# One more slot tile of each destination block fetched from DRAM by node number, with 18 gathered tiles in place of 20

## The chip, the cores and the metric

The kernel runs on one NeuronCore of a Trainium2 chip. The metric is the device time of one execution in microseconds (us), lower is better; the figure is the median of three runs. Beside it stands one execution taken with the hardware profiler, from which every duration comes. TensorE is called PE here, its weight loads PEld; VectorE is DVE, ScalarE is ACT, GpSimd is POOL and SyncE is SP.

## The reference

A graph of 10,000 nodes and 160,000 edges, 128 features a node. Seven propagations (hops) along the edges make seven further tokens of each node, and a small attention block reads the eight tokens out.

```
N, E, D, K = 10000, 160000, 128, 7
h = x; toks = [x]
for _ in range(K):
    msg = h[src] * deg_inv_sqrt[src, None] * deg_inv_sqrt[dst, None]
    h = segment_sum(msg, dst, N)
    toks.append(h)
tok = stack(toks, axis=1)               # (N, 8, D)
# one self-attention block over the 8 tokens of a node (layernorm, q, k, v, softmax, wo, residual),
# then a softmax readout over the tokens with w_r
```

src and dst are drawn at random and uniformly over the nodes.

## The kernel before

**Hops as dense matmuls.** The nodes are cut into 79 blocks of 128. A hop goes over the 79 destination blocks. The edges of one destination block are sorted into cells by the block of their source node; a cell has 32 slots (CAP), a group of four cells makes a slot tile of 128 slots, and 80 cells (NS) make 20 slot tiles (NJ). The edges that don't fit, up to 128 of a destination block, are the left-over edges.

For a destination block t (function `block`), `gather` makes two slot tiles at a time in a PSUM buffer p: for each cell one matmul of a one-hot matrix of 128 x 32 (in w, fp8) against the source block of the table in SBUF (tab, 128 x 256 in f16, the high and low parts of the values). These are L442, eight for a p, 80 for a block; four that lie side by side fill the 128 partitions of a slot tile. ACT or DVE casts p to an SBUF buffer e (L445, ten a block; `evac` says which engine: ACT six and DVE four in hops 2 to 7, ACT all in hop 1). `scat` then adds each slot tile into acc with a one-hot matrix of 128 x 128 (L426, 20 a block).

The left-over edges come another way: POOL issues an indirect DMA (L418), which fetches 128 rows of the table's copy in DRAM (tabd) by the node numbers in oidx into a tile og, and `over` adds it to acc with the one-hot matrix Sov (L432). Then DVE sums the two halves of acc to s (L434) and `fin` runs: in hops 2 to 6 the next table's rows (L559 on ACT, L560 and L562 on DVE) and their write to tabd, issued from ACT's queue (L563), in all hops the scaled token r on POOL (L461) and its write from SP (L463). The fetches of a hop read the whole of the table that the hop before wrote.

**Order.** The program hangs each block's scatters and its `over` on a list `pend` and takes them off two behind, so that the last two scatters and `over` of a block run behind the gathers of the next. The framework then orders the instructions of each engine when the kernel is built, by the program's order and its own estimate of what is ready, and adds all semaphores; an instruction that needs a buffer waits until the buffer's last reader is done. In hops 2 to 7 there are six p buffers, two acc, four og, five w, four s and r; in hop 1 three p, two acc, two og, one s and one r.

**Before and beside hop 1.** Pass A (`pass_a`) sorts the edges into a table TT by destination block (one-hot matrices of 80 columns on DVE, matmuls); `decode` takes the numbers out of TT: kB the cell, sl the node within its source block plus one, dl the destination within its block. In hop 1, `place` sorts the edges of four destination blocks into cells (oh and ux on DVE, 40 pairs of blocks), and `matrices` builds w for each block: DVE compares a broadcast row of source numbers (rb, read back from srow in DRAM) with the partition number for the gather half of w (L403), and the destination numbers dsl with a row of numbers for the scatter half (L406); w is kept in DRAM (GSd) and loaded again in hops 2 to 7 (L568). The matrices of later blocks are built beside hop 1 over the earlier ones.

If an edge is lost, the count of `missing` edges is above zero and a slow path (`slow_hops`, seven loops of 1250 steps with indirect DMAs) computes all tokens anew. After the hops `attention` reads the tokens.

Of the kernel before, what the change touches and what calls it, by code (L numbers as in the profile page):

```python
# [19 lines left out]
NT = 79  # L20
NS = 80
# [4 lines left out]
CAP = 32  # L26
NJ = NS // 4
# [6 lines left out]
class Hops:  # L34
    def __init__(self, ctx, dp, missing, tc, x, src, dst, dis):
# [4 lines left out]
        self.GSd = [dp.tile([128, NJ * 256], F8, name=f"gsd{t}") for t in range(NT)]  # L40
# [3 lines left out]
        self.srow = dp.tile([NS, NS * CAP], F16, name="srow")  # L44
# [48 lines left out]
        self.tab = [cp.tile([128, NS, 256], F16, name=f"tab{i}") for i in range(2)]  # L93
# [7 lines left out]
        self.oidx = cp.tile([128, NT], I32, name="oidx")  # L101
# [116 lines left out]
    def pass_a(self):  # L218
        tc, nc, V, A, T, G = self.tc, self.nc, self.nc.vector, self.nc.scalar, self.nc.tensor, self.nc.gpsimd
        with ExitStack() as c:  # L220
# [33 lines left out]
            for ch in range(NCH):  # L254
                oh, U = st
                U2 = wp.tile([128, NS, 2], F16, name="U2")
                A.activation(U2, U[:, :, None].to_broadcast([128, NS, 2]), AF.Copy)  # L257
# [3 lines left out]
                o12 = w1.tile([128, NP, 2 * NS, 2], F16, name="o12")  # L261
                self.times(o12[:, :, :NS], oh, D1[:, ch])
                self.times(o12[:, :, NS:], oh, D2[:, ch])
# [3 lines left out]
                ta = pp.tile([128, 2, NS], F32, name="ta")  # L267
# [3 lines left out]
                V.tensor_reduce(self.TT[:, ch], ta.rearrange("p h k -> p k h"), axis=X, op=ALU.add)  # L271

    def decode(self):
# [139 lines left out]
    def block(self, t, w, tab, tabd, pend, lag, runs, first, evac, fin):  # L413
# [9 lines left out]
        def scat(e, jj):  # L423
            for j in range(2):
                J = 2 * jj + j
                T.matmul(acc[:, :m], w[:, (NJ + J) * 128:(NJ + J + 1) * 128], e[:, j, :m], start=J == 0, stop=False)  # L426
# [576 lines left out]
```

## Time and profile before

| what | us |
|---|---|
| median of three runs | 4508.32 (4507.62 to 4515.4) |
| the profiled execution, its own time | 4508.36 |
| its span in the trace, first to last instruction | 4506.6 |
| pass A ends, decode begins | 506.2 |
| first gather of hop 1 | 582.6 |
| last matmul of hop 1 | 1370.1 |
| last matmul of hop 7 | 3664.5 |

All stage times are counted from the start of the span. Durations in the text are of this one execution; its own time is 0.04 us from the median. A row of a group reads: line, engine, operation, what is written and read, shapes, count, then busy us and the mean ns of one, then the idle time of the engine ahead of them and what ended it. A timeline row reads: start us, length us, engine, line, operation, count; in brackets the idle time ahead of it and what ended that.

### The profile page before, as it was taken

To read this page: it belongs to the slowest core of one execution; us is meant where nothing else is said; L and a number is where in the kernel's file an instruction comes from. 1 tells how busy PE (TensorE), PEld (TensorE's weight loads), DVE (VectorE), ACT (ScalarE), POOL (GpSimd) and SP (SyncE) were. 2 spreads that over 40 slices of the span, in tenths; PEclk is the share of its full clock that TensorE was granted. 3 is DMA by queue.
4 is the path that set the end of the run, shared out by engine and by line. 5 is a ranking of instruction groups with operands and counts; after the bars stand their busy time and mean duration, and the time that the engine had idled before them with its cause. 6 is when DMAs were issued, how large, how long until landed. Compare 5 with 4: busy or idle time off the path is not lost.

```text
span 4506.6 us, 170913 instructions
## 1 busy us (share of the span) xinstructions
PE 4015.8 (89%) x74352; PEld 3266.3 (72%) x74352; DVE 3529.0 (78%) x7740; ACT 2521.5 (56%) x5159; POOL 1256.0 (28%) x1423
## 2 busy tenths in 40 slices
PE   0566389999998999999999999999999989999996
PEld 0456366766766888888888888888888867777774
DVE  5888799999996777777777777777766668888887
ACT  3000036565666777777777777777766645544542
POOL 0000024334343333333333333333333322222221
PEclk9887689999998999999999999999999989999998
DMA  3000044454455555555555555555555541221210
GB/s 115 1 1 1 1 132 149 140 155 149 142 154 187 182 180 177 183 185 183 178 182 181 179 182 184 177 184 184 181 163 169 164 128 52 65 63 56 65 56 10
DMA packets 296789, 588.20 MB, mean 131 GB/s; under 512 B 46895, under 2 KB 198541, under 8 KB 290781
## 3 DMA queue, kind: packets, MB, share of 16 engines
q1 hardware_dynamic: 218893, 509.90, 34.3%
q0 software_dynamic: 17696, 36.28, 3.8%
q10 hardware_dynamic: 59440, 31.03, 2.4%
q8 instruction: 582, 9.54, 0.8%
q14 instruction: 178, 1.46, 0.1%
HBM read 447.66 MB, written 129.38 MB: 128 GB/s over the span
## 4 chain that ended last, share of the span: by engine, by line
PE 51%; DVE 32%; issue 9%; DMA 4%; POOL 2%; ACT 1%; SPq 1%; ACTq 0%; DVEq 0%; POOLq 0%
PE p L442 20%; PE acc L426 20%; PE ta L270 3%; DVE w L406 3%; DVE st L859 3%; DVE st L856 2%; DVE o L183 2%; DVE w L403 2%; DMA rb<-srow 2%; DVE ro L265 2%; PE tb L335 1%; POOL r L461 1%; DVE R L183 1%; DVE oh L177 1%; DVE ux L190 1%
## 5 line engine op out<-in xcount | busy, mean ns | idle before, releaser
L445 ACT CAST eb<-p 128x512 f16<-128x512 f32 x3634 | 1859.9, 607 | 738.9 <-PE p L442 723.6
L445 DVE CAST eb<-p 128x512 f16<-128x512 f32 x1896 | 1180.2, 683 | 461.3 <-PE p L442 460.7
L442 PE MATMUL p<-tab,w 128*32 128x256 f16 x44240 | 1426.2, 274 | 30.1 <-ACT eb L445 14.3
L426 PE MATMUL acc<-eb,w 128*128 128x256 f16 (+1 forms) x11060 | 1409.4, 274 | 3.1 <-DVE indeg L483 3.0
L442 PEld LDWEIGHTS <-w 128*32 128x32 fp8e4 x44240 | 1118.1, 96 | 268.2 <-issue 185.4
L418 POOL DMA_INDIRECT og<-tabd,oidx x553 | 620.4, 1122 | 2217.8 <-PE acc L432 1426.1
L426 PEld LDWEIGHTS <-w 128*128 128x128 fp8e4 x11060 | 1019.2, 98 | 270.5 <-issue 156.4
L461 POOL TENSOR_SCALAR r<-s,ctok 128x128 f32<-128x128 f32 x553 | 451.2, 816 | 341.4 <-DVE indeg L483 170.5
L560 DVE SCALAR_TENSOR_TENSOR tab<-s,c,tab 128x128 f16<-128x128 f32 x395 | 139.2, 352 | 182.5 <-ACT tab L559 181.1
L434 DVE TENSOR_REDUCE s<-acc 128x128 f32<-128x256 f32 x553 | 234.2, 423 | 41.2 <-PE acc L432 30.7
L406 DVE TENSOR_TENSOR w<-dsl,iof 128x2560 fp8e4<-128x2560 f16 x79 | 222.5, 2816 | 1.2 <-ACT dsl L351 1.2
L257 ACT ACTIVATE U<-U 128x160 f16<-128x160 f32 x25 | 7.6, 304 | 384.5 <-PE U L250 384.5
L768 PEld LDWEIGHTS pv<-Wv,xT 128*128 128x128 f32 x1250 | 165.1, 192 | 75.7 <-issue 57.0
L780 PEld LDWEIGHTS po<-v,pT 128*128 128x128 f32 x1250 | 164.4, 192 | 74.8 <-issue 74.8
L270 PE MATMUL ta<-o,ro 128*128 128x160 f16 x1250 | 132.0, 284 | 93.3 <-DVE ro L265 93.3
L781 ACT COPY o<-po 128x512 f32<-128x512 f32 (+1 forms) x157 | 91.8, 584 | 210.9 <-PE po L780 210.9
L270 PEld LDWEIGHTS <-ro 128*128 128x128 f16 x1250 | 127.0, 121 | 97.4 <-DVE ro L265 97.0
L559 ACT ACTIVATE tab<-s,c 128x128 f16<-128x128 f32 x395 | 158.6, 401 | 62.0 <-DVE s L434 7.4
L748 ACT COPY xT<-pt 128x512 f32<-128x512 f32 (+1 forms) x157 | 91.1, 580 | 166.0 <-PE pt L747 165.9
L768 PE MATMUL pv<-Wv,xT 128*128 128x130 f32 x1250 | 165.8, 276 | 0.0
L780 PE MATMUL po<-v,pT 128*128 128x128 f32 x1250 | 165.1, 275 | 0.0
L250 PE MATMUL U<-oh,tri 128*128 128x80 f16 x1250 | 62.2, 221 | 114.7 <-DVE oh L177 114.7
(245 smaller groups left out, 4291.4 us busy)
## 6 DMA issues: line engine op xcount, KB each, us to landing
w<-gsd SPq DMA_DIRECT2D x474, 640.0 KB
rb<-srow SPq DMA_DIRECT2D x79, 640.0 KB
gsd<-w SPq DMA_DIRECT2D x79, 640.0 KB
tok<-r SPq DMA_DIRECT2D x546, 64.0 KB
x<-tok SPq DMA_DIRECT2D x273, 128.0 KB
tabd<-tab ACTq DMA_DIRECT2D x395, 64.0 KB
og<-tabd,oidx POOLq DMA_INDIRECT x553, 4.0
x<-in_x SPq DMA_DIRECT2D x39, 128.0 KB
```

The source lines that it names most:

```text
L270: T.matmul(ta, ro[:, j, :, i], o12[:, j, :, i], start=j + i == 0, stop=j + i == NP)
L406: V.tensor_tensor(w[:, NJ * 128:].rearrange("p (j d) -> p j d", d=128), dsl[:, g, :, None].to_broadcast([128, NJ, 128]), self.iof1[:, None ...
L418: G.indirect_dma_start(out=og, out_offset=None, in_=tabd, in_offset=bass.IndirectOffsetOnAxis(ap=self.oidx[:, t:t + 1], axis=0))
L426: T.matmul(acc[:, :m], w[:, (NJ + J) * 128:(NJ + J + 1) * 128], e[:, j, :m], start=J == 0, stop=False)
L434: V.tensor_reduce(s, acc[:, 0:256].rearrange("p (h d) -> p d h", h=2), axis=X, op=ALU.add)
L442: T.matmul(p[32 * q:32 * q + 32, j], w[:, s * CAP:(s + 1) * CAP], tab[:, s, :], start=True, stop=True)
L445: (A.copy if evac(jj) else V.tensor_copy)(e[:, :, 0:256], p.rearrange("p j h d -> p j (h d)"))
L461: self.nc.gpsimd.tensor_scalar(r, s, ct[:, t:t + 1], None, op0=ALU.mult)
L559: A.activation(new[:, t, 0:128], s, AF.Copy, scale=c1[:, t:t + 1])
L560: V.scalar_tensor_tensor(new[:, t, 128:256], s, c1[:, t:t + 1], new[:, t, 0:128], op0=ALU.mult, op1=ALU.subtract)
L768: T.matmul(p[:, g - a, :], S[i]["xT"][:, g, :], Wv, start=True, stop=True)
L780: T.matmul(p[:, g - a, :], PT[i % 2][:, g, :], S[i]["v"][:, g, :128], start=False, stop=g == b - 1, skip_group_check=True)
```

## The change

Of the 20 slot tiles of a destination block, 18 (NG) are gathered as before; they hold the source blocks 0 to 71, node numbers below 9216. One tile (NI) holds the remaining 784 nodes in four cells of some 196 nodes, and its rows are fetched from tabd by node number, with an indirect DMA of its own (og0) beside that of the left-over edges (og1). There are so 76 cells, nine gathers and evictions a block, 18 scatters, and a matmul of the fetched tile, `fetched`, which stands behind the block's first scatter, or in `over` for block 0. Its matrix is the 19th of the scatter half of w, which now comes first in w. acc is taken at the first scatter. The og buffers are two of each kind in place of four. In hop 1 `fetched` has a second matmul of one column, which counts degrees. `decode` works out the cell and the node number within it; `place` sums the node numbers of the fetched tile into PSUM with four small matmuls a block and converts them to oidx on DVE. Pass A works with 79 columns (NK). ACT does five evictions of a block, DVE four.

```diff
 NT = 79
-NS = 80
+NG = 18
+NI = 1
+CELL = 334
+NK = 79
 CAP = 32
-NJ = NS // 4
+NJ = NG + NI
+NS = 4 * NJ
...
-        self.GSd = [dp.tile([128, NJ * 256], F8, name=f"gsd{t}") for t in range(NT)]
+        self.GSd = [dp.tile([128, (NJ + NG) * 128], F8, name=f"gsd{t}") for t in range(NT)]
         self.tabd = [dp.tile([NT * 128, 256], F16, name=f"tabd{i}") for i in range(2)]
-        self.srow = dp.tile([NS, NS * CAP], F16, name="srow")
+        self.srow = dp.tile([NTP, 4 * NG * CAP], F16, name="srow")
...
-        self.oidx = cp.tile([128, NT], I32, name="oidx")
+        self.oidx = cp.tile([128, NT, NI + 1], I32, name="oidx")
...
-        m, k = oh.shape[1], 5
-        ux = wu.tile([128, m, NS, 2], F16, name="ux")
-        nc.vector.tensor_tensor(ux, oh, U2[:, None].to_broadcast([128, m, NS, 2]), op=ALU.mult)
+        m, nk, k = oh.shape[1], oh.shape[2], 5
+        ux = wu.tile([128, m, nk, 2], F16, name="ux")
+        nc.vector.tensor_tensor(ux, oh, U2[:, None].to_broadcast([128, m, nk, 2]), op=ALU.mult)
-        for s in range(0, NS, k):
-            T.matmul(R, self.id16, ux[:, :, s:s + k, :], start=s == 0, stop=False, skip_group_check=True)
+        for s in range(0, nk, k):
+            e = min(k, nk - s)
+            T.matmul(R[:, :, :e, :], self.id16, ux[:, :, s:s + e, :], start=s == 0, stop=False, skip_group_check=True)
...
-                oh = self.onehot(wp, "oh", K4[:, ch], NS)
-                U = pp.tile([128, NS], F32, name="U")
+                oh = self.onehot(wp, "oh", K4[:, ch], NK)
+                U = pp.tile([128, NK], F32, name="U")
...
-            t = ep.tile([128, 3, NCH, NTP], I32, name="t")
+            t = ep.tile([128, 5, NCH, NTP], I32, name="t")
+            src, blk, cell, loc, dl = (t[:, i] for i in range(5))
+            n0 = NG * 512
             V.tensor_scalar(vi, self.TT, 1024.0, -1024.0, op0=ALU.mult, op1=ALU.add)
+            V.tensor_single_scalar(dl, vi, 127, op=ALU.bitwise_and)
+            A.activation(self.dl, dl, AF.Copy, bias=1.0)
+            V.tensor_single_scalar(src, vi, 7, op=ALU.arith_shift_right)
+            V.tensor_single_scalar(blk, vi, 14, op=ALU.arith_shift_right)
+
+            V.tensor_scalar(blk, blk, float(4 * NG), None, op0=ALU.min)
+            V.tensor_scalar(cell, src, float(-n0), float(CELL), op0=ALU.add, op1=ALU.mult)
+            V.tensor_single_scalar(cell, cell, 16, op=ALU.arith_shift_right)
+            V.scalar_tensor_tensor(self.kB, cell, 0.0, blk, op0=ALU.max, op1=ALU.add)
+            V.scalar_tensor_tensor(loc, blk, -128.0, src, op0=ALU.mult, op1=ALU.add)
+            A.activation(self.sl, loc, AF.Copy, bias=1.0)
             V.tensor_scalar(self.TT, self.TT, 1024.0, -1023.0, op0=ALU.mult, op1=ALU.add)
-            V.tensor_single_scalar(t[:, 0], vi, 14, op=ALU.arith_shift_right)
-            A.copy(self.kB, t[:, 0])
-            V.tensor_scalar(t[:, 1], vi, 7, 127, op0=ALU.arith_shift_right, op1=ALU.bitwise_and)
-            A.activation(self.sl, t[:, 1], AF.Copy, bias=1.0)
-            V.tensor_single_scalar(t[:, 2], vi, 127, op=ALU.bitwise_and)
-            A.activation(self.dl, t[:, 2], AF.Copy, bias=1.0)
             self.lag_rows(ep, self.kB, self.wB, NCH)
...
-        nc.sync.dma_start(self.srow[a:b, :].rearrange("t (s r) -> s t r", r=CAP), tbs[:, :n, 0:CAP])
+        nc.sync.dma_start(self.srow[a:b, :].rearrange("t (s r) -> s t r", r=CAP), tbs[:4 * NG, :n, 0:CAP])
         for g in range(n):
             for q in range(4):
                 T.matmul(msc[32 * q:32 * q + 32, 32 + g * NJ:32 + (g + 1) * NJ], tbs[:, g, CAP:2 * CAP], self.esel[:, q, :],
                          start=True, stop=True, tile_position=(0, 32 * q))
+                T.matmul(msc[32 * q:32 * q + 32, 16 + g * NI:16 + (g + 1) * NI], tbs[:, g, 0:CAP], self.esel[:, q, NG:],
+                         start=True, stop=True, tile_position=(0, 32 * q))
         A.copy(dsl[:, :n, :], msc[:, 32:32 + n * NJ].rearrange("p (g j) -> p g j", j=NJ))
+        V.tensor_scalar(self.oidx[:, a:b, :NI], msc[:, 16:16 + n * NI].rearrange("p (g i) -> p g i", i=NI), float(NG * 512 - 1), None, op0=ALU.add)
...
-        V.scalar_tensor_tensor(self.oidx[:, a:b], l3[:, :n, 0], 128.0, l3[:, :n, 1], op0=ALU.mult, op1=ALU.add)
+        V.scalar_tensor_tensor(self.oidx[:, a:b, NI], l3[:, :n, 0], 128.0, l3[:, :n, 1], op0=ALU.mult, op1=ALU.add)
...
-            w = self.gsp.tile([128, NJ * 256], F8, name="w")
-            V.tensor_scalar(w[:, :NJ * 128], rb, self.pid1, None, op0=ALU.is_equal, saturate=False)
+            w = self.gsp.tile([128, (NJ + NG) * 128], F8, name="w")
+            V.tensor_scalar(w[:, NJ * 128:], rb, self.pid1, None, op0=ALU.is_equal, saturate=False)
             if t != ts[-1]:
                 rb = row(t + 1)
-            V.tensor_tensor(w[:, NJ * 128:].rearrange("p (j d) -> p j d", d=128), dsl[:, g, :, None].to_broadcast([128, NJ, 128]),
+            V.tensor_tensor(w[:, :NJ * 128].rearrange("p (j d) -> p j d", d=128), dsl[:, g, :, None].to_broadcast([128, NJ, 128]),
                             self.iof1[:, None, :].to_broadcast([128, NJ, 128]), op=ALU.is_equal, saturate=False)
             nc.sync.dma_start(self.GSd[t], w)
...
-    def block(self, t, w, tab, tabd, pend, lag, runs, first, evac, fin):
+    def block(self, t, w, tab, tabd, pend, lag, runs, first, evac, fin, drain=True):
 
         nc, V, A, T, G = self.nc, self.nc.vector, self.nc.scalar, self.nc.tensor, self.nc.gpsimd
-        acc = self.pacc.tile([128, 512], F32, name="acc", tag="acc")
-        og = self.ogp.tile([128, 256], F16, name="og")
-        G.indirect_dma_start(out=og, out_offset=None, in_=tabd,
-                             in_offset=bass.IndirectOffsetOnAxis(ap=self.oidx[:, t:t + 1], axis=0))
+        og = []
+        for i in range(NI + 1):
+            o = self.ogp.tile([128, 256], F16, name=f"og{i}")
+            G.indirect_dma_start(out=o, out_offset=None, in_=tabd,
+                                 in_offset=bass.IndirectOffsetOnAxis(ap=self.oidx[:, t, i:i + 1], axis=0))
+            og.append(o)
         m = 257 if first else 256
+        acc = []
 
 
         def scat(e, jj):
-            for j in range(2):
+            if not acc:
+                acc.append(self.pacc.tile([128, 512], F32, name="acc", tag="acc"))
+            for j in range(e.shape[1]):
                 J = 2 * jj + j
-                T.matmul(acc[:, :m], w[:, (NJ + J) * 128:(NJ + J + 1) * 128], e[:, j, :m], start=J == 0, stop=False)
+                T.matmul(acc[0][:, :m], w[:, J * 128:(J + 1) * 128], e[:, j, :m], start=J == 0, stop=False)
+                if J == 0 and t > 0:
+                    fetched()
+
+
+        def fetched():
+            for i in range(NI):
+                W = w[:, (NG + i) * 128:(NG + i + 1) * 128]
+                T.matmul(acc[0][:, :256], W, og[i], start=False, stop=False)
+                if first:
+                    T.matmul(acc[0][:, 256:257], W, self.ones16, start=False, stop=False)
 
         def over():
+            if t == 0:
+                fetched()
             So = self.Sov[:, t, :]
             if first:
-                T.matmul(acc[:, 256:257], So, self.ones16, start=False, stop=False)
-            T.matmul(acc[:, :256], So, og, start=False, stop=True)
+                T.matmul(acc[0][:, 256:257], So, self.ones16, start=False, stop=False)
+            T.matmul(acc[0][:, :256], So, og[NI], start=False, stop=True)
             s = self.fp.tile([128, 128], F32, name="s")
-            V.tensor_reduce(s, acc[:, 0:256].rearrange("p (h d) -> p d h", h=2), axis=X, op=ALU.add)
-            fin(t, s, acc)
+            V.tensor_reduce(s, acc[0][:, 0:256].rearrange("p (h d) -> p d h", h=2), axis=X, op=ALU.add)
+            fin(t, s, acc[0])
 
         def gather(jj):
+            n = min(2, NG - 2 * jj)
             p = self.pg.tile([128, 2, 2, 128], F32, name="p")
-            for j in range(2):
+            for j in range(n):
                 for q in range(4):
                     s = 4 * (2 * jj + j) + q
-                    T.matmul(p[32 * q:32 * q + 32, j], w[:, s * CAP:(s + 1) * CAP], tab[:, s, :], start=True, stop=True)
+                    T.matmul(p[32 * q:32 * q + 32, j], w[:, NJ * 128 + s * CAP:NJ * 128 + (s + 1) * CAP], tab[:, s, :], start=True, stop=True)
             e = self.ebuf[self.eb_i % len(self.ebuf)]
             self.eb_i += 1
-            (A.copy if evac(jj) else V.tensor_copy)(e[:, :, 0:256], p.rearrange("p j h d -> p j (h d)"))
-            pend.append(lambda: scat(e, jj))
+            (A.copy if evac(jj) else V.tensor_copy)(e[:, :n, 0:256], p[:, :n].rearrange("p j h d -> p j (h d)"))
+            pend.append(lambda: scat(e[:, :n], jj))
 
         jj = 0
-        for n in runs:
+        for i, n in enumerate(runs):
             for _ in range(n):
                 gather(jj)
                 jj += 1
-            while len(pend) > lag:
+            while drain and len(pend) > lag:
                 pend.pop(0)()
-            if n is runs[-1] and jj == NJ // 2:
+            if i == len(runs) - 1:
                 pend.append(over)
             yield
+            G.memset(self.TT[:, :, NK:], 0.0)
...
+                    yield from self.block(t, w, self.tab[0], self.tabd[0], pend, 2, (2, 2, 2, 3), True, lambda jj: True, fin1)
 
...
-            self.ogp = c.enter_context(tc.tile_pool(name="og2", bufs=4))
+            self.ogp = c.enter_context(tc.tile_pool(name="og2", bufs=2))
...
-                    w = self.gsp.tile([128, NJ * 256], F8, name="w")
+                    w = self.gsp.tile([128, (NJ + NG) * 128], F8, name="w")
                     nc.sync.dma_start(w, self.GSd[t])
-                    for _ in self.block(t, w, tab, din, pend, 2, (10,), False, lambda jj: jj % 5 in (0, 2, 4), fin):
+                    for _ in self.block(t, w, tab, din, pend, 2, (9,), False, lambda jj: jj in (0, 2, 4, 5, 7), fin):
```

More of the change, by code (lines that the diff above doesn't have):

```diff
@@ L91, in __init__ @@
         V.tensor_mul(self.dis2, self.disT, self.disT)
-        self.tab = [cp.tile([128, NS, 256], F16, name=f"tab{i}") for i in range(2)]
+        self.tab = [cp.tile([128, NTP, 256], F16, name=f"tab{i}") for i in range(2)]
         self.indeg = cp.tile([128, NT], F32, name="indeg")
@@ L255, in pass_a @@
                 oh, U = st
-                U2 = wp.tile([128, NS, 2], F16, name="U2")
-                A.activation(U2, U[:, :, None].to_broadcast([128, NS, 2]), AF.Copy)
+                U2 = wp.tile([128, NK, 2], F16, name="U2")
+                A.activation(U2, U[:, :, None].to_broadcast([128, NK, 2]), AF.Copy)
                 if ch + 1 < NCH:
@@ L266, in pass_a @@
                                 self.io2[:, None].to_broadcast([128, NP, 128, 2]), op=ALU.is_equal)
-                ta = pp.tile([128, 2, NS], F32, name="ta")
+                ta = pp.tile([128, 2, NK], F32, name="ta")
                 for j in range(NP):
@@ L492, in hop1 @@
                 for t, w in zip(quads[q], W[q]):
-                    yield from self.block(t, w, self.tab[0], self.tabd[0], pend, 2, (2, 3, 2, 3), True, lambda jj: True, fin1)
+                    yield from self.block(t, w, self.tab[0], self.tabd[0], pend, 2, (2, 2, 2, 3), True, lambda jj: True, fin1)
             for _ in self.place(quads[0], dsl[0]):
```

12 lines of the change are left out of this document (6 added, 6 removed).

## The prediction

> **What bounds the kernel now.** I read the page first: the engines' busy shares, then the chain that ended last.
>
> ```profile
> PE 4015.8 (89%) x74352; PEld 3266.3 (72%) x74352; DVE 3529.0 (78%) x7740; ACT 2521.5 (56%) x5159; POOL 1256.0 (28%) x1423
> PE 51%; DVE 32%; issue 9%; DMA 4%; POOL 2%; ACT 1%; SPq 1%; ACTq 0%; DVEq 0%; POOLq 0%
> ```
>
> These are averages over stages with different limits, so I then took windows: a stretch of hop 1 (which also builds the matrices), hop 4, and the last hop. Columns: window, its us, busy us of each engine, granted TensorE clock, DMA share, GB/s.
>
> ```profile
> 785.00:985.00 200.00, 184.58 (x3221) 137.88 (x3221) 193.88 (x271) 119.80 (x254) 80.18 (x40) 0.97 0.46 146
> 2149.80:2527.10 377.30, 376.13 (x7986) 317.95 (x7986) 274.77 (x565) 271.53 (x553) 128.40 (x158) 1.00 0.57 181
> 3281.50:3665.00 383.50, 380.51 (x7979) 317.34 (x7977) 230.48 (x398) 240.04 (x475) 128.40 (x158) 1.00 0.50 159
> ```
>
> Hop 1 is DVE's (97%). Hops 2 to 7, six windows of 368 to 384 us, are PE's (99%) at full clock; DVE and ACT are at 73%, POOL at 34%. One block there, from the timeline (start, length, engine, line):
>
> ```profile
> 2002.07 2.42 PE L442 MATMUL p<-tab,w 128*32 128x256 f16 x80
> 2002.53 3.03 ACT L445 CAST eb<-p 128x512 f16<-128x512 f32 x6 [1.16 <-PE p L442]
> 2002.74 2.48 DVE L445 CAST eb<-p 128x512 f16<-128x512 f32 x4 [0.80 <-PE p L442]
> 2004.42 0.61 PE L426 MATMUL acc<-eb,w 128*128 128x256 f16 x4
> 2004.87 0.27 PE L432 MATMUL acc<-og,Sov 128*128 128x256 f16 x1
> 2004.98 1.91 PE L426 MATMUL acc<-eb,w 128*128 128x256 f16 x16
> 2005.25 0.42 DVE L434 TENSOR_REDUCE s<-acc 128x128 f32<-128x256 f32 x1
> 2005.42 1.01 POOL L418 DMA_INDIRECT og<-tabd,oidx  x1 [3.07 <-PE acc L432]
> 2006.46 0.62 POOL L461 TENSOR_SCALAR r<-s,ctok 128x128 f32<-128x128 f32 x1
> 2006.52 0.33 ACTq L563 DMA_DIRECT2D tabd<-tab  x1
> 2006.81 2.13 PEld L442 LDWEIGHTS <-w 128*32 128x32 fp8e4 x80 [0.21 <-issue]
> ```
>
> The period is 2006.81 - 2002.07 = 4.74 us: 20 groups of four gather matmuls in 2.13, 0.21 idle, 21 matmuls of scatter shape in 2.18, 0.21 idle. So a group of four costs 0.107, a scatter 0.104, and each change between the two kinds of matmul 0.21. Nothing waits for the fetch, issued four blocks ahead.
>
> **Hops 2 to 7, steady part.** A block loses two groups of four and two scatters, and gains one matmul on the fetched tile: 41 slots become 38. 2 x 0.107 + 0.104 = 0.318; two changes of kind remain. 6 x 79 = 474 blocks x 0.318 = **-150.7 us**, a period of 4.43.
>
> Will the others keep up? ACT loses its sixth eviction and would be next to bound. Its last work is the write's issue (L563), which ends 4.78 after the block's start; that hangs on s, which follows the same four DVE evictions, so it doesn't move. The next block's first eviction is wanted 0.46 after its start, 4.43 + 0.46 = 4.89: 0.11 of margin, where 0.42 is left now. DVE is free at 4.62 and wanted at 5.10. POOL has 2 x 1.01 + 0.62 = 2.64 of 4.43.
>
> The fetches have less lead: two buffers each instead of four. A tile's first matmul in block t frees the buffer for t+2, two periods ahead, 8.85 us. But on POOL both fetches and r come ready within about 1 us: the second fetch of one block is freed by L432, the first of the next by the fetched matmul two slots later, r by s. So a fetch can be issued up to 1.8 after its buffer is free (an issue of 1.01, its gap of 0.3, part of r's 0.62), and the lead is 7.05. Nothing else queues on POOL; a late r delays only SP's tok write, which has four buffers. Landing in these hops:
>
> ```profile
> DMA to landing us min/median/max: 3.2/4.0/6.1
> ```
>
> So it is hidden, with 0.95 to spare at the maximum. SP's w load shrinks (to 37/40); acc keeps its two buffers and is only taken later: both cost nothing, since no wait on either shows inside a hop.
>
> **Hop boundaries.** The new hop's fetches wait for the last table write. Hop 3:
>
> ```profile
> 2151.45 0.33 ACTq L563 DMA_DIRECT2D tabd<-tab  x1
> 2155.85 1.01 POOL L418 DMA_INDIRECT og<-tabd,oidx  x1 [4.86 <-PE p L442]
> 2157.16 0.95 POOL L418 DMA_INDIRECT og<-tabd,oidx  x1 [0.30 <-PE acc L426]
> 2158.42 0.95 POOL L418 DMA_INDIRECT og<-tabd,oidx  x1 [0.30 <-PE p L442]
> 2159.20 0.27 PE L432 MATMUL acc<-og,Sov 128*128 128x256 f16 x1
> ```
>
> Now block 0 needs the first fetch. After, its end (L432) needs the second, 1.31 later, and block 1's fetched matmul, 0.2 behind it, the third, 2.57 later: 2.4 lost, and the 0.5 that shorter gathers had won before it. 2.9 x 6 = **+17.4**; between 6 x 1.3 = 8 and 25.
>
> That idle time may also halve the clock. At hop 2's start PE waited 2.83 and 2.85 us, and then:
>
> ```profile
> 1404.10:1408.00 3.90, 3.90 (x72) 2.63 (x71) 3.13 (x7) 2.65 (x5) 2.10 (x3) 0.50 0.49 77
> ```
>
> Clock 0.50, 71 matmuls in 3.55 instead of 1.89, and 0.5 more on the scatters behind: 2.2 lost. After the single wait of 2.49 at hop 7's start nothing was lost (80 in 2.20). The four middle boundaries will wait about 2.1 (0.16 now, as L432 starts 0.61 and not 0.45 behind the scatters of 2158.59; + 1.31 + 0.6) and then 1.1, nearest to the row of 2.49, which lost nothing; hop 7's will wait 4.4 and 1.1, nearest to hop 2's. 0 to 11; I take hop 7's and one in four of the rest, **+4**. The Trainium skill ("TensorE: Matmul & The Clock Gate", Why this matters for your kernels) warns against PE gaps of over about 3 us between bursts of matmuls, since one idle window brings the half clock back; the trace of hop 2 agrees. By it I would charge all five boundaries, 11 us, and forecast 7 more.
>
> **Hop 1 and the matrices.** DVE sets the pace, and its tiles shrink with their elements:
>
> ```profile
> L406 DVE TENSOR_TENSOR w<-dsl,iof 128x2560 fp8e4<-128x2560 f16 x79 | 222.5, 2816 | 1.2 <-ACT dsl L351 1.2
> L403 DVE TENSOR_SCALAR w<-rb,pid 128x2560 fp8e4<-128x2560 f16 x79 | 122.2, 1547 | 16.7 <-DMA rb<-srow 16.7
> ```
>
> L406 2560 to 2432: 79 x 0.141 = 11.1. L403 2560 to 2304: 79 x 0.155 = 12.2. oh and ux of 80 to 76 columns: 40 x (0.112 + 0.112) = 9.0. New: the conversion of the node numbers, 20 x 0.165 (L382's size) = 3.3. Net 29. PE and ACT shed work too; the tiny matmuls that sum the node numbers and the one-column degree matmul lie on PE beside it. Against it: POOL issues are slower here (1.82 us mean, r 2.01), and s and r have one buffer each, so a late r holds DVE's next s. POOL would have 2 x 1.82 + 2.01 = 5.65 of 7.3, the tightest spacing of blocks seen (s at 1115.62 and 1122.88). If 20 blocks held DVE for 2 us each, 40 would go: between -29 and +11. I take **-25**, near the first, as mean POOL load fits. The Trainium skill ("GPSIMD Engine Reference", 8. Key points) says that GpSimd shares its SBUF interfaces with VectorE, which speaks against work on POOL here; the stretched issues agree (1.82 against 1.01), while DVE's oh takes 2.25 here against 2.235 with POOL idle.
>
> **Before hop 1.** Pass A with 79 columns for 80: four DVE groups of 2.23 x 25 x 1/80 = **-2.8**, all of it on the path, where DVE and PE take turns. Decode gets three more tensor_scalars (spaced 1.13) and two scalar_tensor_tensors of 2000 elements (L145's 1.53 for 1280 gives 2.3), on DVE ahead of all else: **+8**. The memset of the unused column runs on POOL, idle until 585, at no cost. The attention after 3665 isn't touched.
>
> **Sum**, against the profiled execution, 4508.36 (span 4506.6; the median of the three runs, 4508.32, is the same): -150.7 + 17.4 + 4 - 25 - 2.8 + 8 = -149, **4359**. A saving in proportion (3/41 of 4.74 = 0.347) with the best ends gives about 4328; hop 1 at +11 and the full boundaries 4410.
>
> **Rivals.**
> *ACT becomes the bound.* The 0.11 margin fails and a block takes 4.55: 474 x 0.12 = 57 more, 4416. For: the margin is thin. Against: with six p buffers the seventh gather tile (1.28 after the block's start) needs an eviction that ends at 1.07, so ACT may slip 0.2 before PE waits.
> *Late fetch, slower.* A fetch's loop is 1.8 + landing L over two blocks: it costs from L = 7.05, and the sum turns slower from about 7.7. At 8.9, the longest landing in hop 1, the period is 5.35: 474 x 0.61 - 20 + 21 = +290, 4798. For: twice the fetches, half the buffers. Against: 6.1 was the longest here.
> *More changes of kind on PE.* At boundaries the order on PE departs from the program's (gathers of block 1 run before block 0's scatters). If the fetched matmul broke one burst a block, two more changes, 0.42 x 474 = 199: 4558.
> *It doesn't do what it says.* 196 nodes per 32-slot cell overflow more; past 128 left-over edges in a block the slow path would run, 7 x 1250 steps of at least two landings of 3.1, over 54,000 us. Counted from the drawn indices, the fullest block has 116 (70 now).
>
> **Chances.** Forecast 0.73, ACT 0.15, late fetch 0.05, more changes 0.05, slow path 0.01, no change 0.01. 0.2% is 9 us, about what a measurement of this kernel can tell: faster 0.88, same 0.01, slower 0.11. The range takes the forecast's bounds and the ACT case: 4330 to 4435.
>
> **What would show it.** Period 4.43 in hops 2 to 7 with 72 gathers in 1.92 and two 0.21 gaps; L432 waiting 2 to 3 us for the fetch at each hop's start; no wait inside a hop; L406 at 2.68, L403 at 1.39. Waits on og inside hops, a third 0.21 per block, or DVE waiting for r in hop 1 would prove it wrong.

## The result, and the profile after

The changed kernel takes **4351.56 us** (median of 4 runs, 4347.68 to 4356.03) against 4511.13 of the kernel before beside it (4 runs): a ratio of 0.9646, 95% interval 0.9629 to 0.9663. The prediction was 4359, in a range of 4330 to 4435. The profiled execution took 4351.51, with a span of 4349.7: 156.9 shorter than the span before.

The page of the changed kernel: engines, then the chain that ended last.

```profile
PE 3825.1 (88%) x69770; PEld 3101.5 (71%) x69770; DVE 3464.2 (80%) x7765; ACT 2250.6 (52%) x4605; POOL 1859.9 (43%) x1977
PE 56%; DVE 33%; DMA 4%; issue 2%; POOL 1%; ACT 1%; SPq 1%; ACTq 1%; DVEq 0%; POOLq 0%
```

PE has 4582 matmuls fewer, POOL 600 us more. The windows that answer to those of before (a stretch of hop 1, hop 4, hop 7; columns as there):

```profile
785.00:985.00 200.00, 178.73 (x3145) 132.07 (x3145) 187.74 (x279) 111.09 (x235) 115.59 (x60) 0.97 0.43 140
2088.20:2440.80 352.60, 348.24 (x7274) 293.60 (x7271) 267.56 (x565) 232.74 (x474) 203.64 (x237) 1.00 0.63 197
3149.60:3504.90 355.30, 348.64 (x7270) 294.18 (x7268) 223.41 (x397) 201.52 (x396) 203.63 (x237) 0.99 0.55 176
```

Hops 4 and 7 are 353 and 355 us long, 377 and 384 before, and PE is now idle 4.4 to 6.7 us of each: they still are PE's. In hop 1 DVE went from 97% to 94% busy: there something else began to hold it. One block of hop 3 from the timeline:

```profile
1965.50 0.33 ACTq L597 DMA_DIRECT2D tabd<-tab  x1
1965.53 1.87 PEld L475 LDWEIGHTS <-w 128*32 128x32 fp8e4 x72 [0.21 <-issue]
1965.55 0.94 POOL L434 DMA_INDIRECT og<-tabd,oidx  x1 [0.30 <-issue]
1965.98 2.54 ACT L478 CAST eb<-p 128x512 f16<-128x512 f32 x5 [0.90 <-PE p L475]
1967.61 0.61 PE L446 MATMUL acc<-eb,w 128*128 128x256 f16 x4
1968.06 0.27 PE L464 MATMUL acc<-og,Sov 128*128 128x256 f16 x1
1968.28 0.27 PE L454 MATMUL acc<-og,w 128*128 128x256 f16 x1
1968.39 1.58 PE L446 MATMUL acc<-eb,w 128*128 128x256 f16 x13
1969.90 0.34 PEld L475 LDWEIGHTS <-w 128*32 128x32 fp8e4 x16 [0.21 <-issue]
```

The period is 1969.90 - 1965.53 = 4.37, with 72 gathers (L475), 18 scatters (L446), the left-over tile (L464), the fetched tile (L454, which stands among the scatters) and two gaps of 0.21 (the one ahead of the gathers is in brackets; the other lies between their last weight load, which ends at 1967.40, and the scatters at 1967.61).

By stage; a hop ends with its last left-over matmul (L432 before, L464 after). Where hop 1 alone is given below, it runs from its first such matmul to its last (778.0 before, 766.4 after):

| stage | before | after | difference | predicted |
|---|---|---|---|---|
| start to decode | 506.2 | 499.1 | -7.0 | -2.8 |
| decode, to the first one-hot of hop 1 | 40.0 | 47.6 | +7.6 | +8 |
| from there through hop 1 | 824.0 | 813.6 | -10.4 | -25 |
| hops 2 to 7 | 2294.4 | 2144.5 | -149.9 | -129 |
| after hop 7 | 842.1 | 844.8 | +2.8 | 0 |
| sum | | | -156.9 | -149 |

### The profile page after: what moved, and what is told of

It is laid out like the page before. It is cut to its first block, busy times and chain, and to the rows that moved or that the text cites. A ratio compares the mean times of both kernels' runs of the same rounds, so it can differ in the third digit from the quotient of the medians.

```text
span 4349.7 us, 162150 instructions
## 1 busy us (share of the span) xinstructions
PE 3825.1 (88%) x69770; PEld 3101.5 (71%) x69770; DVE 3464.2 (80%) x7765; ACT 2250.6 (52%) x4605; POOL 1859.9 (43%) x1977
## 4 chain that ended last, share of the span: by engine, by line
PE 56%; DVE 33%; DMA 4%; issue 2%; POOL 1%; ACT 1%; SPq 1%; ACTq 1%; DVEq 0%; POOLq 0%
PE acc L446 23%; PE p L475 23%; PE ta L275 3%; DVE w L421 3%; DVE st L893 3%; DVE st L890 2%; DVE o L187 2%; DVE w L418 2%; DVE oh L181 2%; DMA rb<-srow 2%; DVE ro L270 1%; DVE R L187 1%; DMA og<-tabd,oidx 1%; DVE ux L194 1%; PE acc L454 1%
## 5 line engine op out<-in xcount | busy, mean ns | idle before, releaser
L478 ACT CAST eb<-p 128x512 f16<-128x512 f32 x3081 | 1593.8, 603 | 706.3 <-PE p L475 675.8
L434 POOL DMA_INDIRECT og<-tabd,oidx x1106 | 1202.3, 1087 | 1646.5 <-PE acc L454 650.1
L446 PE MATMUL acc<-eb,w 128*128 128x256 f16 (+1 forms) x9954 | 1355.6, 276 | 10.8 <-DVE indeg L517 8.3
L475 PE MATMUL p<-tab,w 128*32 128x256 f16 x39816 | 1288.7, 276 | 34.8 <-ACT eb L478 18.1
L475 PEld LDWEIGHTS <-w 128*32 128x32 fp8e4 x39816 | 1007.2, 97 | 235.1 <-issue 172.2
L446 PEld LDWEIGHTS <-w 128*128 128x128 fp8e4 x9954 | 916.9, 98 | 277.4 <-issue 169.3
L421 DVE TENSOR_TENSOR w<-dsl,iof 128x2432 fp8e4<-128x2432 f16 x79 | 211.8, 2681 | 0.0
L275 PE MATMUL ta<-o,ro 128*128 128x158 f16 x1250 | 126.6, 277 | 87.5 <-DVE ro L270 87.5
L865 POOL TENSOR_TENSOR p<-e,in 128x512 f32<-128x512 f32 (+1 forms) x40 | 40.8, 1019 | 377.3 <-DVE e L863 377.3
L454 PE MATMUL acc<-og,w 128*128 128x256 f16 x553 | 151.7, 274 | 17.8 <-DMA og<-tabd,oidx 17.8
```

What stands on the lines that cost most here:

```text
L275: T.matmul(ta, ro[:, j, :, i], o12[:, j, :, i], start=j + i == 0, stop=j + i == NP)
L421: V.tensor_tensor(w[:, :NJ * 128].rearrange("p (j d) -> p j d", d=128), dsl[:, g, :, None].to_broadcast([128, NJ, 128]), self.iof1[:, None ...
L434: G.indirect_dma_start(out=o, out_offset=None, in_=tabd, in_offset=bass.IndirectOffsetOnAxis(ap=self.oidx[:, t, i:i + 1], axis=0))
L446: T.matmul(acc[0][:, :m], w[:, J * 128:(J + 1) * 128], e[:, j, :m], start=J == 0, stop=False)
L454: T.matmul(acc[0][:, :256], W, og[i], start=False, stop=False)
L475: T.matmul(p[32 * q:32 * q + 32, j], w[:, NJ * 128 + s * CAP:NJ * 128 + (s + 1) * CAP], tab[:, s, :], start=True, stop=True)
```

## The experiments

**Theory.** In hops 2 to 7 the gain is matmul slots on PE, less what the fetches cost at each hop's start: POOL issues them one by one, some 1.25 apart, PE waits for the second and the third, and the granted clock halves behind it. In hop 1 the shorter DVE work is lost to new waits. **Rivals:** the fetch also slows the steady blocks; the boundary loss is the table write's, not the fetch's; hop 1's loss is that POOL and DVE disturb each other at the SBUF, or POOL's load as such.

The runs fell on four chips. Those of one group below ran on the same chip, beside runs of the kernel before: 4515.9 us on chip A, 4512.1 on B, 4512.3 on C, 4520.1 on D.

### Chip A: no fetch, a later matmul, one buffer, r on ACT

**No fetch in hops 2 to 7** (the edges of the fetched tile are left out there).

```diff
         for i in range(NI + 1):
+            if i < NI and not first:
+                og.append(None)
+                continue
...
         def fetched():
-            for i in range(NI):
+            for i in range(NI if first else 0):
```

> The changed kernel with the node-number fetch (og0) and its matmul left out of hops 2 to 7 only; hop 1 keeps both. It leaves out the edges of the fetched tile in those hops. Theory (the gain is matmul slots on PE; the fetch costs its own slot in every block, and at a hop's start one more serial issue on POOL, a wait of PE for the third fetch and the half clock behind it): the steady period falls from 4.37 to 4.265 (474 x 0.105 = 50 us) and the boundaries give back about 25 to 35 us, so some 4270 us; the granted clock at the hop starts stays at 1.00 but for hop 2 and hop 7. Rival A (late fetch: waiting or traffic of the fetches also slows the steady blocks): the period falls below 4.25 and the total below 4250. Rival B (the boundary losses are the table write and the clock, not the fetch): only the 50 us come, some 4300.

Measured 4263.8 (ratio 0.9445, 0.943 to 0.9459). A block takes 4.26 (gathers start at 2060.46 and 2064.72), and hops 2 to 7 take 2066.1, which is 76 less than the 2142.4 of the changed kernel in a later run of it on chip B: 474 x 0.11 = 52 in the steady blocks and 24 at the boundaries. So, against that run, the fetch costs its slot on PE and the boundaries, and nothing else in a block. Rivals A and B fall. The total is 89 less than the changed kernel's on chip B, since hop 1, which this edit leaves alone, took 744.8 here and 767.4 there; chip C's section comes back to it.

**Block 1's fetched matmul in `over`, one og buffer, hop 1's r on ACT**, three kernels:

```diff
-                if J == 0 and t > 0:
+                if J == 0 and t > late:          # late = 0 in hop 1, 1 in hops 2 to 7
...
-            if t == 0:
+            if t <= late:
```

> The changed kernel with the fetched matmul of block 1, like that of block 0, put into the end of the block (over) in hops 2 to 7; nothing is left out. Theory (at a hop's start PE waits 1.1 to 1.6 us for the second fetch and 1.9 to 2.4 for the third, and the two together bring the half clock): the wait for the third goes, since it is then wanted one period later, and the clock stays at 1.00 at most boundaries: 10 us from the wait and up to 15 from the clock, 4327 to 4342 us. Rival (the wait only moves, since the end of block 1 then needs the third and the fourth fetch, issued 1.25 us apart, and the clock halves all the same): 4346 to 4354, with waits of 1 to 2 us at the end of block 1.

```diff
-            self.ogp = c.enter_context(tc.tile_pool(name="og2", bufs=2))
+            self.ogp = c.enter_context(tc.tile_pool(name="og2", bufs=1))
```

> The changed kernel with one og buffer of each kind in hops 2 to 7 in place of two. It tests the loop of the late-fetch rival: a fetch can be issued when the tile's last matmul frees the buffer and is wanted one period later. Theory: the loop (0.2 to the issue, up to 1.25 behind the other fetch, 2.85 to 4.1 to the landing, 0.27 for the matmul) is longer than 4.37, so every block waits for a fetch: period 4.7 to 5.8, I take 5.1, so 474 x 0.73 = 346 us more, some 4700 us, with the granted clock falling where waits repeat. With two buffers the same loop has two periods, 8.74, which is why no wait shows. Rival (the fetch is not near any limit): no change, 4352.

```diff
-        self.nc.gpsimd.tensor_scalar(r, s, ct[:, t:t + 1], None, op0=ALU.mult)
+        if k == 1:
+            self.nc.scalar.activation(r, s, AF.Copy, scale=ct[:, t:t + 1])
+        else:
+            self.nc.gpsimd.tensor_scalar(r, s, ct[:, t:t + 1], None, op0=ALU.mult)
```

> The changed kernel with hop 1's scaled token r worked out on ACT in place of POOL; hops 2 to 7 as they are. Theory (in hop 1 r is late, since POOL now has two fetches a block; SP's tok write waits for r, and behind it on SP's queue stands the read of the row rb, for which DVE then waits): the waits of the row compare for rb fall from 27 us to below 12, r is never waited for, hop 1 gains 10 to 17 us, 4335 to 4342. Rival A (the row is late because of its own two trips to DRAM and back): rb waits stay at 20 to 27 and the time at 4349 to 4354. Rival B (POOL and DVE share a path to SBUF): DVE's groups themselves get shorter by over 1%, beside the waits. Rival C (ACT's casts of the gathered tiles are delayed and PE with them): slower, above 4356.

Measured 4704.7, 4779.9 and 4705.1: all far slower. For the one-buffer kernel the theory had said some 4700, but most of its loss is one that the other two share, and that neither theory nor rival had. The r edit touches hop 1 alone, yet its hops 2 to 7 took 2521.9, 5.19 a block. A block of it, from the timeline:

```profile
2062.73 1.10 PEld L475 LDWEIGHTS <-w 128*32 128x32 fp8e4 x43 [0.21 <-issue]
2062.75 0.95 POOL L434 DMA_INDIRECT og<-tabd,oidx  x1 [0.30 <-issue]
2063.55 0.59 ACT L478 CAST eb<-p 128x512 f16<-128x512 f32 x1 [1.15 <-PE p L475]
2064.27 0.35 PEld L475 LDWEIGHTS <-w 128*32 128x32 fp8e4 x14 [0.44 <-issue]
2064.33 2.48 DVE L478 CAST eb<-p 128x512 f16<-128x512 f32 x4 [1.35 <-PE p L475]
```

The gathers start together with POOL's second fetch issue, as in the changed kernel. But the first cast starts 0.82 behind them, not 0.45, and DVE's first 1.60, not 0.67; then PE itself stands 0.44 (the row names no releaser, but it is the seventh tile of p that starts late, and there are six buffers). The matmuls look regular, since their ends are modelled; their semaphores in the trace show the first tile of p done at 0.80 in place of 0.43, the second at 1.59 in place of 0.65, the ninth at 3.00 in place of 2.18. The third to the sixth follow the second 0.09 to 0.10 apart, where a tile otherwise takes 0.22. So part of the delay may lie in the news of finished work and not in the work; no run here tests that. Where the second issue came before the gathers, in some blocks of the one-buffer kernel, the first tile was on time and the second again late:

```profile
2065.06 0.94 POOL L434 DMA_INDIRECT og<-tabd,oidx  x1 [0.30 <-issue]
2065.68 2.33 PE L475 MATMUL p<-tab,w 128*32 128x256 f16 x72
2066.13 2.66 ACT L478 CAST eb<-p 128x512 f16<-128x512 f32 x5 [1.42 <-PE p L475]
2066.65 2.48 DVE L478 CAST eb<-p 128x512 f16<-128x512 f32 x4 [1.36 <-PE p L475]
```

In both, DVE's first cast starts 1.58 and 1.59 after POOL's second issue, wherever the gathers stand. Without the fetch, on this chip too, the only issue of a block lies beside the scatters, and the gathers run as usual.

### Chip B: the changed kernel again, and both edits together

> The changed kernel itself, as it is. In the three kernels that still fetch the tile and were run together (block 1's fetched matmul moved; one og buffer; r on ACT), the ninth gather tile of a block is ready 3.0 us after the block's first gather, not 2.18, in the same instruction order on PE: the first p comes at 0.81 in place of 0.43, the second at 1.59 in place of 0.65, whenever POOL's second fetch issue starts with the gathers. Without the fetch (same chip) the gathers are as before. Theory C (the chip: on some chips POOL's issue of a fetch holds up what PE finishes beside it): on the chip where those kernels were run this one takes 4700 too; on the first chip 4352. Theory D (the build: something in those three kernels' programs): 4352 on any chip.

> The changed kernel with both edits: r of hop 1 on ACT and block 1's fetched matmul in over in hops 2 to 7. Where the gathers run as in the changed kernel's first profile, hop 1 is 10 to 20 us shorter and each of the hops 3 to 7 is 2 to 5 us shorter: 4315 to 4335 beside 4352. Under theory C it is slow exactly where the changed kernel beside it is slow (about 4690 beside 4700), under theory D it is slow alone.

The changed kernel took 4352.6 (0.9647, 0.9634 to 0.966) and both edits together **4296.4** (0.9522, 0.9509 to 0.9535), 56 less, and neither had the slow gathers. The two edits gained more than I had expected (4315 to 4335).

### Chip C: each edit alone, and the queue of SP

> The kernel with hop 1's r on ACT once more (it took 4705 on the chip of the first four runs, where the changed kernel itself was not run; the changed kernel took 4353 and both edits together 4296 on another). Theory C (that chip holds up the gathers beside POOL's second issue): on any other chip the ninth gather tile is ready at 2.18 and the kernel takes 4352 less its own gain in hop 1. Theory D (this program): 4700 again. Its own gain, with the waits for rb down from 28 to 4 to 6 us: 20 to 36 us of the 56 of both edits, 4317 to 4332.

> The kernel with block 1's fetched matmul in over once more. Theory C as for the run beside it: 4352 less its own gain at the hop boundaries on any chip but the first one of these experiments; theory D: 4700 again. Its own gain: hops 3 to 7 took 349 to 352 in the run with both edits and 353 to 355 in the changed kernel, so 18 to 22 us, 4330 to 4335; one matmul wait of about 1.3 us on og at each hop's start, none of 2, and the granted clock above 0.9 there.

Measured 4311.7 (0.9559, 0.9546 to 0.9572) and 4337.8 (0.9613, 0.96 to 0.9626), the one 5 below and the other 3 above what I had expected. These are the programs that had taken 4705 on chip A: theory C holds, theory D falls. Each chip was seen on one occasion only, so what belongs to the chip and what to the occasion is not told apart. In the r kernel here, with POOL's second issue at the same place:

```profile
2029.81 1.87 PEld L475 LDWEIGHTS <-w 128*32 128x32 fp8e4 x72 [0.21 <-issue]
2029.83 0.94 POOL L434 DMA_INDIRECT og<-tabd,oidx  x1 [0.30 <-issue]
2030.27 2.05 ACT L478 CAST eb<-p 128x512 f16<-128x512 f32 x4 [0.90 <-PE p L475]
2030.49 1.89 DVE L478 CAST eb<-p 128x512 f16<-128x512 f32 x3 [0.54 <-PE p L475]
```

Against the changed kernel on chip B, r on ACT shortens hop 1 by 36.2 (767.4 to 731.2), and the later matmul shortens hops 2 to 7 by 16.7 (2142.4 to 2125.7). The stages that an edit leaves alone differ by 1.2 and 2.9 between the chips; within one chip r on ACT is worth 36.4 on B (767.4 to 731.0 in the kernel with both edits) and 33.3 on C (against the 764.5 of the kernel with the later matmul).

How the boundary works, in the changed kernel (start of hop 5) and with both edits (the same start):

```profile
2447.20 1.01 POOL L434 DMA_INDIRECT og<-tabd,oidx  x1 [4.95 <-PE p L475]
2448.52 0.94 POOL L434 DMA_INDIRECT og<-tabd,oidx  x1 [0.30 <-issue]
2449.76 0.94 POOL L434 DMA_INDIRECT og<-tabd,oidx  x1 [0.30 <-PE acc L446]
2451.39 0.27 PE L464 MATMUL acc<-og,Sov 128*128 128x256 f16 x1 [1.07 <-DMA og<-tabd,oidx]
2454.19 0.37 PE L454 MATMUL acc<-og,w 128*128 128x256 f16 x1 [2.42 <-DMA og<-tabd,oidx]
...
2454.10:2458.00 3.90, 3.81 (x30) 2.44 (x33) 0.00 (x0) 0.07 (x1) 1.98 (x3) 0.50 0.26 75
```

```profile
2405.65 0.27 PE L455 MATMUL acc<-og,w 128*128 128x256 f16 x1 [0.45 <-DMA og<-tabd,oidx]
2406.78 0.27 PE L465 MATMUL acc<-og,Sov 128*128 128x256 f16 x1 [0.87 <-DMA og<-tabd,oidx]
2408.51 2.15 PE L476 MATMUL p<-tab,w 128*32 128x256 f16 x72
```

Three issues 1.32 and 1.24 apart: the end of block 0 waits 1.07 for the second, the fetched matmul of block 1 another 2.42 for the third, and the next 3.9 us run at a granted clock of 0.50 (the window, last line of the first fence). With the edit the second wait is gone at this place and the next 72 gathers take 2.15, so the clock stayed up; a wait of 0.99 for a later fetched tile follows 10 us on. It didn't go so at every start: in the kernel with the later matmul alone the end of block 0 waited 2.37 at the start of hop 6, and the clock halved there and at hop 7's start, against my expectation of waits near 1.3 and a clock above 0.9.

**Hop 1's tok write from POOL's queue**, r left on POOL:

```diff
-        self.nc.sync.dma_start(self.tok[k][t * 128:t * 128 + n, :], r[:n])
+        (self.nc.gpsimd if k == 1 else self.nc.sync).dma_start(self.tok[k][t * 128:t * 128 + n, :], r[:n])
```

> The changed kernel with hop 1's tok write issued from POOL's queue behind r, in place of SP's; r stays on POOL and as late as before, and POOL gets one more issue a block. Theory (SP's queue: the tok write waits there for the late r, and the read of rb stands behind it): DVE's waits for rb fall from 28 us to below 8 though POOL is busier, and hop 1 gains 10 to 30 us, 4322 to 4342. Rival (POOL's load as such delays what DVE needs, r on ACT helped by taking load off it): the waits for rb stay, the fetches come later, hop 1 is the same or longer, 4350 to 4370.

Measured 4319.2 (0.9574, 0.9561 to 0.9587), hop 1 741.1: 26 less than the changed kernel on chip B, 23 less than the unedited hop 1 on this chip, with POOL busier. The total is 3 below what the theory had. Its groups (row compare on DVE, r and the write on POOL):

```profile
L418 DVE TENSOR_SCALAR w<-rb,pid 128x2304 fp8e4<-128x2304 f16 x79 | 112.9, 1430 | 4.8 <-DMA rb<-srow 4.8
L494 POOL TENSOR_SCALAR r<-s,ctok 128x128 f32<-128x128 f32 x76 | 176.9, 2327 | 93.4 <-DVE indeg L517 60.7 <-DVE po L379 18.2 <-DMA tok<-r 7.2
L496 POOL DMA_DIRECT2D tok<-r x76 | 54.4, 716 | 22.2 <-POOL r L494 22.1
```

In the changed kernel the same row compare, and the order of the queues in one group of four blocks:

```profile
L418 DVE TENSOR_SCALAR w<-rb,pid 128x2304 fp8e4<-128x2304 f16 x79 | 112.4, 1423 | 27.0 <-DMA rb<-srow 27.0
...
725.94 0.32 SPq L357 DMA_DIRECT2D srow<-tbs  x1
726.11 1.01 POOL L434 DMA_INDIRECT og<-tabd,oidx  x1 [2.07 <-PE acc L446]
726.51 0.42 DVE L466 TENSOR_REDUCE s<-acc 128x128 f32<-128x256 f32 x1
727.47 2.80 POOL L494 TENSOR_SCALAR r<-s,ctok 128x128 f32<-128x128 f32 x1 [0.36 <-DMA tok<-r]
730.30 0.33 SPq L496 DMA_DIRECT2D tok<-r  x1
730.73 5.64 SPq L411 DMA_DIRECT2D rb<-srow  x2
734.60 1.42 DVE L418 TENSOR_SCALAR w<-rb,pid 128x2304 fp8e4<-128x2304 f16 x1 [2.17 <-DMA rb<-srow]
```

DVE has s done at 726.93; POOL is in a fetch issue until 727.12, its r waits 0.35 more (by the row for the last tok write, since r has one buffer) and takes 2.80; SP's tok write waits for r; the read of the row rb stands behind it on SP and goes out 4.79 after srow's write did; DVE waits 2.17. In nine of the twenty groups the read left 4.76 to 5.05 after srow's write, in the others mostly 1.5 to 1.8. Before it was 1.6 in the median and never over 4.4, with the same write between in eleven groups; with the write off SP's queue it is 1.5 to 1.65 but for two. r itself stayed as slow (2327 ns), so it is the queue, not POOL's load: the theory holds. DVE's waits for the left-over digits (L397, 13.6 us in the changed kernel) fell to 0.6 with it.

The loss is not the same on every chip. Four kernels on chips A and D leave hop 1 as it is in the changed kernel, with the same order of instructions on every engine (no fetch, the later matmul and one buffer on A, one buffer on D). Their hop 1 took 744.8, 754.7, 756.3 and 746.1, DVE waited 6.1 to 11.8 for rb, and at most two reads in twenty left more than 4.7 after srow's write. There r on ACT won little or nothing: 746.1 on chip A. So the two fetches alone don't make r late enough to cost much; what else does on chips B and C was not found.

### Chip D: one buffer, a copy on ACT, the kernel before with r on ACT

> The kernel with one og buffer of each kind in hops 2 to 7 once more, on a chip where the gathers run at 2.18. The loop of the late-fetch rival with one period in place of two: the fetch is issued when the tile's last matmul frees the buffer and is wanted 4.37 us later. Theory: the loop (0.3 to 1.6 to the issue, 2.85 to 4 to the landing, 0.27 for the matmul) is longer than 4.37 in most blocks; PE waits for og inside the hops, period 4.6 to 5.3, 4480 to 4750 us, I take 4600. So two buffers are needed and two are enough. Rival (a fetch is never near a limit): 4352, no waits inside a hop.

```diff
-                V.tensor_copy(self.indeg[:, t:t + 1], acc[:, 256:257])
+                A.copy(self.indeg[:, t:t + 1], acc[:, 256:257])
```

> Both edits (r of hop 1 on ACT, block 1's fetched matmul in over) and the copy of the degree column in hop 1 on ACT in place of DVE. Theory (hop 1 is DVE's: with the waits for rb gone, DVE work that goes comes back one to one): 79 copies of 0.147 = 11.6 us less on DVE, 4283 to 4290 beside 4296. Rival (DVE's waits for ACT grow, since s, r and the copy are queued behind the casts there): 4294 to 4305.

The r edit in the kernel before:

> The kernel before, with hop 1's r on ACT in place of POOL and nothing else. Theory (the change's 29 us of DVE work in hop 1 were lost in part to the queue on SP; before had 16.7 us of the same waits): its waits for rb fall below 6, hop 1 gains 8 to 16 us, 4496 to 4504; against it the changed kernel with the same edit (4312) is then 185 to 192 shorter, of which 25 to 32 in hop 1. Rival (before gains as much as the changed kernel did, 36 us): 4476, and the change then saves nothing in hop 1 beyond its 10 us.

Measured 4776.2, 4712.6 and 4528.6. The first two kernels had the slow gathers (second p at 1.6, ninth at 3.0), so chip D is like A, and their totals say nothing of their edits. What one buffer costs in hops 2 to 7 is best read on chip A, where the r kernel differs from it in hop 1 and the buffers alone: 61.1 us (2583.0 against 2521.9). On chip D it is 71.8 (2585.3 against 2513.5), but the kernel beside it has the later matmul too, which is worth 10.4 on chip A (2521.9 to 2511.5). On chip D PE and POOL wait for og 146 times (112.1 us) where two buffers have 13 waits (11.3). So with one buffer the fetch is late at a period of 5.2 to 5.4 already, and two are needed; what it would cost at 4.37 was not seen. Whether the copy on ACT helps stays open: hop 1 took 761.8, with DVE waiting 18.3 for ACT's dsl ahead of L366, which favours its rival, and the unedited hop 1 on this chip took 746.1; but no kernel beside it differs by this copy alone.

The kernel before lost by its edit: ratio 1.0019 (1.001 to 1.0028), 8.5 us slower, and its waits for rb stayed (20.6, where its first profile has 16.7). My expectation failed. In the first profile of the kernel before r was seldom in the read's way (the read left 1.6 after srow's write in the median), which fits. But on chip A the same edit won nothing clear in the changed kernel either, so this run doesn't settle what it would do on chips B and C. That the late reads came with the change rests on the first profiles: none over 4.4 before, nine over 4.7 after.

## Why the prediction was right, point by point

- **The total was near in part by luck.** -149 was predicted and -156.9 came, but the terms were off by -33 (steady blocks), +13 (boundaries), +15 (hop 1), -4 (ahead of decode) and +3 (after hop 7, which no edit touches), and these errors mostly cancel.
- **Steady blocks: the term was too small.** Predicted 4.43 and -150.7; measured 4.37, which over full hops (79 x 4.745 or, in hop 7, 4.81, against 79 x 4.37) is -184. The scatters and the gaps cost what I took. But the 80 gathers of before held a small wait: by their starts in the trace, nine tiles of p follow each other every 0.218, before as after, and the tenth came 0.257 behind the ninth, 0.326 in hop 7. There are six p buffers, so that the tenth tile takes the buffer of the fourth, whose eviction was just ending. From first to last start the burst was 2.144 and is 1.876: 0.268 gone, where I had 2 x 0.107 = 0.214, read off a burst whose end was slower than its beginning. That the eviction is what the tenth waited for is read from the buffer count, and was not tried.
- **Boundaries: the mechanism was right, the size too small.** Predicted +21.4 with the clock; hops 2 to 7 measure -149.9 against -184, so +34. PE waited for the two fetches that I had named, but I had the longer wait at the second (2.1, then 1.1 for the third, in hops 3 to 6), and it came at the third: 1.07 to 1.6, then 1.85 to 2.42 (so my sign, L432 waiting 2 to 3, was not met). Their sum, 3.2 to 3.7 in those hops, is near the 3.2 told. The clock halved at all five later boundaries, for 3.4 to 10.2 us, not at two. I took a single wait of 2.49 that had lost nothing as the nearest row; two waits within 4 us are another case. By the rule of the Trainium skill ("TensorE: Matmul & The Clock Gate", Why this matters for your kernels) I would have charged 11 for the clock and not 4, which was nearer, although at four of the five starts no single gap was over 2.42.
- **Hop 1: the step that failed.** DVE's work fell by 28.6 (772.57 to 743.96 in the two windows), as the sum of 29 had it, but only 10.4 came, since DVE's idle time grew by 18.2 (51.6 to 69.8), 10.3 of it in the waits for rb (16.7 to 27.0). I named what was queued on SP in hops 2 to 7 ("a late r delays only SP's tok write") and did not ask it for hop 1, where the read of rb is behind that write. The risk that I did weigh, r holding DVE's next s, was 0.4 us. With r on ACT 33 to 36 us more come on chips C and B, twice what the change had added to DVE's idle time, so waits that the kernel before had go too (DVE is idle 35.9 with both edits on chip B). On chips A and D most of the loss isn't there to begin with.
- **Pass A, decode.** Decode cost +7.6 for +8. The stretch before it won 7.0 for 2.8: DVE's work there fell by 2.6, as told, and its waits by the other 4.4; why was not looked for.
- **The rivals.** ACT did not become the bound: its write's issue ends at 1965.83 and its next cast starts at 1965.98, 0.15 apart where I had 0.11. No fetch was late inside a hop (all 16 waits of PE on og in hops 2 to 7 are at the hops' starts, 25.5 us). The fetched matmul broke no burst: two gaps a block. The slow path did not run.
- **What no rival had:** on chips A and D kernels with the two fetches take some 4700. The changed kernel itself was not run there; that it would be slower than before on them is concluded from the programs that ran on A and on C.

The version with both edits, 4296.4, beats both kernels, on a chip without the slow gathers.

## What to carry to other kernels

Before you price a burst by its length over its count, look whether its last part is slower than its first: there a wait for a buffer hides, and removing work removes that as well. For an engine that gets later, list what stands behind each instruction that waits for it, on every queue and in every stage, not only in the stage you think of. Where a new stage begins with several transfers from one issuing engine, count which of them the first users need, and let a user that can wait stand one step later.

## What the runs showed of the hardware that was not expected

- The same program takes 4705 us on one chip and 4312 on another; the kernel before differs by under 0.2% (4512 to 4520). On the slow ones, chips A and D, PE's gathers finish late beside POOL's second fetch issue (second p 1.58 after the issue's start), 0.82 us a block. Whether the issue itself holds PE, or what it starts, could not be told apart, nor whether it is the chip or the occasion.
- Two PE waits of 1.07 and 2.42 us with 0.4 us of work between them brought the granted clock to 0.50; one of 2.49 alone (the kernel before), and 0.45 with 0.87, did not. But one of 2.37 alone did (the later matmul, hop 6), so the length of a wait doesn't decide it. In these traces the clock changes at steps of 3.41 us. Of such stretches at full clock in hops 2 to 7 of all fourteen profiles, each of the 50 in which PE stood idle, by its rows, for 58% or more was followed by one at 0.50, and none of the 9185 with 46% or less was; the 26 between went both ways. Here it was the idle share of such a stretch that counted.
- DVE's durations hardly depended on POOL: on chip B POOL is busy 277 us in hop 1 with both edits in place of 458, and L194 takes 2130 ns in place of 2128, L421 2683 in both, the row compare L418 1417 in place of 1428 and the one-hot oh (L181) 2130 in place of 2149. By the Trainium skill ("GPSIMD Engine Reference", 8. Key points) the two share their SBUF interfaces; these DVE groups show a cost of less than 1%.
